# Moving a four-tile TensorE block to the head of the output product, with one wait ahead of it and two PSUM banks for its remainder

## Chip, cores, metric

One core of one Trainium2 chip (trn2). The metric is the device time of one execution in microseconds. Faster or slower needs 2%; smaller differences are given with their 95% interval.

## The reference

An attention without a score matrix, then a dense layer with a gated activation, for 8 batches, 8 heads, 576 positions, 64 channels a head, 2048 hidden units:

```python
q_s = softmax(q, channels); k_s = softmax(k, positions)
kv  = einsum('bhsd,bhse->bhde', k_s, v)          # a 64 x 64 matrix per head
x   = einsum('bhsd,bhde->bhse', q_s, kv)         # 576 x 64 per head
h   = x @ w_in                                   # 4608 x 512 by 512 x 2048
out = (h * sigmoid(beta * h)) @ w_out            # 4608 x 2048 by 2048 x 512
```

## The kernel before

The kernel works in nine slabs of 512 rows. Slab t is batch t's first 512 positions; slab 8 collects the remainders (64 positions of each of 8 batches). A slab has **pass one** (16 tiles of four 128x512 matmuls; ScalarE empties each tile's bank with the activation, into GT) and then the **output product** (seven parts of sixteen 128x256 matmuls, a Strassen-like scheme whose partial results VectorE adds up in TS). While slab t runs, TensorE also computes the next slab's x. Time is counted in slots, 64 for each of the two passes.

From slab 3 on, the next batch's x comes from `quad`: 64x64 matmuls in the four quarters of the array at once. It has eight matmuls of 512 columns (`x_mm`, for XT) and, for batches 6 and 7, sixteen of 64 columns for the remainders of a pair of batches (`r_mm`, for XT8). Four banks take the first, one bank both halves (`a` = 0, 1) of the second.

```python
HB, OB, MB = (0, 1, 2), (3, 4), (5, 6, 7)      # PSUM banks; pass one rotates over HB

def quad(b, pi=None):
    bks = list(MB) + [HB[(hrot[0] + 1) % 3], HB[(hrot[0] + 2) % 3]]
    b_r = bks[4]
    ...
    def r_mm(a):
        for g, e_, c in ...:
            op = add(PE, ...matmul into PS[b_r]..., r=[("kvd", d, hp), "qtr"], bank=[b_r])
            ...
                op.hard = [o_ for a_, o_ in done if a_ != a]   # TensorE waits for itself
    x_mm(0, 1); r_mm(0); x_mm(0, 0); x_mm(1, 1); x_mm(1, 0); r_mm(1)
    ...  # VectorE and ScalarE copy two banks each to XT; VectorE copies the remainder to XT8

def attn(b):                                    # slabs 4 to 6, b = t + 1
    return [(24 if b == 5 else 16, steps(kv_all, b)),
            (90, one(quad, b, b - 4 if b > 5 else None))]      # third part of the product

def pass2_fast(t, tick, hooks):
    s, z5, z2 = HB[hrot[0] % 3], OB[0], OB[1]
    ...
    at(0)
    ...  # part 1 into bank s, part 2 into bank 3; TS = s; TS -= bank 3   (lines L899, L902)
    prod(z2, *gs2(1), *wo(0, 0), True)                         # part 3 into bank 4
    ...  # TS -= bank 4 (L908), then the other four parts, which use banks 3 and 4 in turn
```

`add` records an operation with the keys it reads and writes and the banks it touches, and gives it a wait for each last operation of another engine on these. The waits of one operation stand ahead of it in its engine's queue.

The softmax here doesn't subtract the row's maximum and nothing guards it: scores larger than these inputs give would overflow.

## Time and profile before

| | |
|---|---|
| time, median of 6 runs | 273.88 us (273.44 to 274.79) |
| span in the profile | 271.7 us |
| TensorE busy | 97%, granted clock 1.00 |
| the block and the waits that it causes, slabs 3 to 6 | 4.30 us |

The last row is worked out in the prediction: in each slab the time from the end of the product's matmuls ahead of the block to the next product matmul, and the two waits for L908. This "block cost" is the measure used below. TensorE is the bound, its matmuls start every 0.109 us (256 columns) or 0.216 us (512 columns), and whatever is longer between two starts is cost.

How to read the profile lines below: a line of a timeline gives start and duration in us, engine, line of the kernel, operation, output and inputs, shape, and how many instructions it holds; in brackets, how long the engine was idle before it and what released it. A line of a list of waits gives the total in us, the number of waits, and the longest. Some traces lack matmul records: that of the kernel before has 1918 of 1937, and a gap of 0.22 us where pass one begins is the time of one 512-column matmul whose record is missing.

### The profile page before, as it was taken

The numbers are of one execution on the slowest core, as the hardware profiler recorded it, in microseconds if no ns is written. First come the engines' busy times: TensorE is split into PE (matmuls) and PEld (weight loads), VectorE is DVE, ScalarE is ACT, GpSimd is POOL, SyncE is SP. The second block draws the span as 40 slices with busy tenths as digits, with TensorE's granted clock in tenths as the row PEclk, the third lists the DMA queues.
The fourth block names the chain that finished last, engine by engine and source line by source line (L and its number), as shares of the span: only waits on it lengthen the run. The fifth ranks groups of instructions, "written<-read, shape, count | busy, mean of one in ns | idle before, by whom it ended". The sixth has DMA issues, their size and how long they took to land.

```text
span 271.7 us, 4870 instructions
## 1 busy us (share of the span) xinstructions
PE 264.3 (97%) x1918; PEld 164.7 (61%) x1937; DVE 192.4 (71%) x408; ACT 181.1 (67%) x286; POOL 62.1 (23%) x80
## 2 busy tenths in 40 slices
PE   8999999999999999999999999999999999999994
PEld 2544454448844885477547864677457745874683
DVE  4964586887867799869776976678686649625762
ACT  4998658789287957897778847883783387018610
POOL 2790010006530099001900570126000100000000
PEclk9999999999999999999999999999999999999999
DMA  7999999989799139920499999112600030012005
GB/s 214 321 204 207 227 326 349 291 231 367 175 340 271 78 62 298 339 80 2 97 315 262 315 330 200 74 29 50 214 0 2 19 157 0 0 60 96 0 3 154
DMA packets 59366, 45.93 MB, mean 169 GB/s; under 512 B 28608, under 2 KB 58320, under 8 KB 58320
## 3 DMA queue, kind: packets, MB, share of 16 engines
q1 hardware_dynamic: 54480, 40.90, 53.0%
q0 software_dynamic: 4240, 4.19, 9.3%
q10 hardware_dynamic: 624, 0.53, 0.6%
q8 instruction: 15, 0.25, 0.4%
q14 instruction: 7, 0.06, 0.1%
HBM read 36.71 MB, written 9.44 MB: 170 GB/s over the span
## 4 chain that ended last, share of the span: by engine, by line
PE 88%; DVE 5%; DMA 2%; SPq 2%; issue 1%; ACT 0%
PE PS L406 51%; PE PS L830 35%; DMA VF<-in_v_dram 2%; PE PS L482 1%; PE PS L543 1%; DVE QS L357 1%; SPq L278 1%; SPq L290 1%; DVE EQ L361 1%; DVE XT L573 1%; DVE VB L377 1%; DVE TS L908 0%; DVE XT L579 0%; DVE QI L359 0%; DVE XT L511 0%
## 5 line engine op out<-in xcount | busy, mean ns | idle before, releaser
L406 PE MATMUL PS<-XT,WIN 128*128 128x512 bf16 x562 | 126.0, 379 | 1.1 <-issue 0.3
L730 ACT ACTIVATE GT<-PS,BETA 128x512 bf16<-128x512 f32 x144 | 95.2, 690 | 37.7 <-PE PS L406 37.4
L406 PEld LDWEIGHTS PS<-XT,WIN 128*128 128x128 bf16 x576 | 55.3, 98 | 64.6 <-DVE XT L511 0.6
L753 DVE TENSOR_SCALAR GT<-GT,RB 128x512 bf16<-128x512 bf16 x144 | 53.3, 392 | 36.3 <-ACT GT L730 35.5
L361 POOL TENSOR_TENSOR EQ<-EQ,QI 128x1024 bf16<-128x1024 bf16 (+1 forms) x13 | 25.6, 1967 | 50.6 <-DVE QI L359 50.0
L830 PE MATMUL PS<-WOUT,GT 128*128 128x256 bf16 x256 | 32.2, 273 | 0.4 <-DVE TS L908 0.4
L830 PE MATMUL PS<-WOUT,GS 128*128 128x256 bf16 x256 | 31.3, 273 | 0.0
L830 PE MATMUL PS<-WSUM,GT 128*128 128x256 bf16 x256 | 30.1, 273 | 0.3 <-DMA QT<-EQ 0.2
L830 PEld LDWEIGHTS PS<-WSUM,GT 128*128 128x128 bf16 x256 | 24.8, 98 | 3.9 <-issue 0.9
L830 PEld LDWEIGHTS PS<-WOUT,GT 128*128 128x128 bf16 x256 | 24.7, 98 | 3.6 <-DVE TS L908 0.9
L866 ACT COPY O2S<-PS 128x512 f32<-128x512 f32 (+1 forms) x17 | 9.4, 561 | 26.2 <-PE PS L830 25.0
L830 PEld LDWEIGHTS PS<-WOUT,GS 128*128 128x128 bf16 x256 | 24.3, 98 | 3.3 <-issue 0.4
L319 ACT ACTIVATE EQ<-QF 128x512 bf16<-128x512 f32 x32 | 18.0, 621 | 7.6 <-DMA QF<-in_q_dram 7.5
L789 DVE TENSOR_TENSOR GS<-GT 128x512 bf16<-128x512 bf16 (+2 forms) x32 | 21.9, 685 | 0.0
L357 DVE TENSOR_REDUCE QS<-EQ 128x16 f32<-128x1024 bf16 (+1 forms) x20 | 19.7, 985 | 0.8 <-ACT EQ L319 0.8
L796 DVE TENSOR_TENSOR GT<-GT 128x2048 bf16<-128x2048 bf16 x16 | 19.8, 1262 | 0.0
L377 POOL CAST VB<-VF 128x512 bf16<-128x512 f32 x24 | 14.8, 616 | 21.9 <-DVE GS L789 13.2
L319 ACT ACTIVATE EK<-KF 128x512 bf16<-128x512 f32 x32 | 18.1, 621 | 0.1
L878 DVE TENSOR_TENSOR O2S<-TS,PS 128x512 f32<-128x512 f32 (+1 forms) x17 | 10.7, 643 | 8.7 <-PE PS L830 8.7
L830 PE MATMUL PS<-WSUM,GS 128*128 128x256 bf16 x128 | 16.6, 273 | 0.0
L406 PE MATMUL PS<-WOUT,GT 128*128 128x512 bf16 x62 | 15.0, 379 | 0.1
L784 DVE TENSOR_TENSOR GS<-GT 128x256 bf16<-128x256 bf16 (+2 forms) x32 | 13.6, 426 | 1.1
(90 smaller groups left out, 215.8 us busy)
## 6 DMA issues: line engine op xcount, KB each, us to landing
out_dram<-O2S SPq DMA_DIRECT2D x8, 1024.0 KB, 5.0
QF<-in_q_dram SPq DMA_DIRECT2D x6, 1024.0 KB, 6.3
KF<-in_k_dram SPq DMA_DIRECT2D x6, 1024.0 KB, 8.7
VF<-in_v_dram SPq DMA_DIRECT2D x6, 1024.0 KB, 12.1
KF<-in_k_dram SPq DMA_DIRECT2D x8, 256.0 KB, 5.6
VF<-in_v_dram SPq DMA_DIRECT2D x8, 256.0 KB, 5.6
WOUT<-in_moe_w_out_dram POOLq DMA_DIRECT2D x4, 512.0 KB, 16.4
WIN<-in_moe_w_in_dram POOLq DMA_DIRECT2D x3, 512.0 KB, 9.2
```

Source lines behind the costliest of these rows:

```text
L319: add(ACTE, lambda e, o=o, a=a: e.activation(o, a, ACT.Exp), r=[(name + "f", i, hp)], w=[("e" + name, i, hp)])
L357: add(DVE, lambda e: e.tensor_reduce(s_, a, AX.X, ALU.add), r=ks, w=[("qs", i, hp0)])
L361: add(eng, lambda e: e.tensor_tensor(a, a, vb, ALU.mult), r=ks + [("qi", i, hp0)], w=ks)
L377: add(eng, lambda e: (e.copy if eng == ACTE else e.tensor_copy)(o, a), r=[("vf", i, hp), ("vone", i)], w=[("vb", i, hp)], after=after)
L406: add(PE, lambda e: e.matmul(o, l, r_, start=start, stop=stop), r=r, w=w, bank=[bk])
L730: add(ACTE, lambda e: e.activation(GT[:, f, :], PS[bk][:, :], ACT.Silu, scale=BETA[:, f:f + 1]), r=[("ps", bk), "beta"], w=[("gt", f, 0), ...
L753: add(DVE, lambda e: e.tensor_scalar(GT[:, f, :], GT[:, f, :], RB[:, f:f + 1], None, ALU.mult), r=k + ["rb"], w=k)
L784: add(DVE, lambda e: e.tensor_tensor(GS1[:, i:i + n, :], gv(i, 0, n), gv(i + NG, 1, n), ALU.add), r=gk(i, 0, n) + gk(i + NG, 1, n), w=[("g ...
L789: add(DVE, lambda e: e.tensor_tensor(GS2[:, i:i + n, :], GT[:, i:i + n, :], GT[:, i + NG:i + NG + n, :], ALU.add), r=[k_ for f in (i, i + ...
L796: add(DVE, lambda e: e.tensor_tensor(gv(f, th, NG), gv(f, th, NG), gv(f, 1 - th, NG), ALU.subtract), r=gk(f, 0, NG) + gk(f, 1, NG), w=gk(f ...
L830: add(PE, lambda e, l=l, r_=r_, st=st, u=u, i=i, b_=b_: e.matmul(PS[b_][:, 256 * u:256 * u + 256], l, r_, start=st, stop=end and i == NG - ...
L878: add(DVE, lambda e, b_=b_, u0=u0, u1=u1: e.tensor_tensor(o[:, u0:u1, :], ts[:, u0:u1, :], bank3(b_)[:, u0:u1, :], ALU.add), r=["ts", ("ps ...
```

## The change

Its intent: let the block stand where two passes meet anyway; replace the waits scattered over its matmuls by one; and give each remainder half its own bank, so that TensorE does not wait for itself. The core of the diff:

```diff
-        def quad(b, pi=None):
-            bks = list(MB) + [HB[(hrot[0] + 1) % 3], HB[(hrot[0] + 2) % 3]]
-            b_r = bks[4]
+        def quad(b, gs=(0, 1), pi=None):
+            bks = list(MB) + [HB[(hrot[0] + 1) % 3], HB[(hrot[0] + 2) % 3], OB[1]]
+            b_r = bks[4:6]
+            used = list(b_x.values()) + (b_r if rem else [])
+            first = [dict(r=[... all kvd, qt, qtr keys of the block ...], bank=used)]
+            def tile(o, l, r_, a, c, bk, keys):
+                kw = dict(r=keys, bank=[bk])
+                if first:
+                    kw = first.pop()            # the first matmul waits for everything
...
-            x_mm(0, 1); r_mm(0); x_mm(0, 0); x_mm(1, 1); x_mm(1, 0); r_mm(1)
+            r_mm(1); x_mm(0, 0); x_mm(0, 1); x_mm(1, 0); x_mm(1, 1); r_mm(0)
+            r_evac(1) ... XT copies ... r_evac(0)
...
-                    (90, one(quad, b, b - 4 if b > 5 else None))]
...
+            if 3 < t < 7:
+                quad(t + 1, (0, 1), t - 3 if t > 4 else None)
             at(0)
```

(Some statements are joined on one line here.) The rest of the diff regroups two steps of slabs 1 and 2 without changing the order of instructions, and splits the key of XT8 in two.

## The prediction

> **What bounds the kernel now.** I read the page first, for shares, then the list of waits, then the order of time around each 64x64 block. Line L406 is pass one (and other full-array matmuls), L830 the output product, L543 the block's 512-column matmuls, L554 its 64-column remainders.
>
> ```profile
> span 271.7 us, 4870 instructions
> PE 264.3 (97%) x1918; PEld 164.7 (61%) x1937; DVE 192.4 (71%) x408; ACT 181.1 (67%) x286; POOL 62.1 (23%) x80
> PE 88%; DVE 5%; DMA 2%; SPq 2%; issue 1%; ACT 0%
> PE PS L406 51%; PE PS L830 35%; DMA VF<-in_v_dram 2%; PE PS L482 1%; PE PS L543 1%; DVE QS L357 1%; SPq L278 1%; SPq L290 1%; DVE EQ L361 1%; DVE XT L573 1%; DVE VB L377 1%; DVE TS L908 0%; DVE XT L579 0%; DVE QI L359 0%; DVE XT L511 0%
> ```
>
> TensorE is busy 97% and holds 88% of the chain that ended last; the block holds 1%. So a change is worth what it alters in the times from one TensorE matmul to the next. The list of TensorE's waits after 100 us holds one that the change can touch; the second list is the weight loads', 125 to 215 us:
>
> ```profile
> PE PS L830 <- DVE TS L908: 0.4, 2, 0.2
> ...
> PEld PS L554 <- PE PS L543: 0.9, 2, 0.5
> ```
>
> The first is the product waiting for VectorE's subtraction from bank 4 (slabs 5 and 6). The second is the remainder's second half waiting on TensorE itself. Slab 5 in order of time shows both (the third line is of the weight loads, the rest of the matmuls):
>
> ```profile
> 177.81 1.04 PE L830 MATMUL PS<-WOUT,GS 128*128 128x256 bf16 x8
> 178.78 0.40 PE L543 MATMUL PS<-QT,KVD 64*64 64x512 bf16 x2
> ...
> 179.51 0.20 PEld L554 LDWEIGHTS PS<-QTR,KVD 64*64 64x64 bf16 x8 [0.47 <-PE PS L543]
> ...
> 179.76 0.39 PE L830 MATMUL PS<-WOUT,GS 128*128 128x256 bf16 x2
> 179.99 1.91 PE L830 MATMUL PS<-WOUT,GT 128*128 128x256 bf16 x16
> 182.08 1.92 PE L830 MATMUL PS<-WOUT,GT 128*128 128x256 bf16 x16 [0.18 <-DVE TS L908]
> ```
>
> The durations overlap in the pipeline, so I use start to start. Twelve product matmuls from 173.66 to 174.97 make 0.109 us each; pass one's take 0.216.
>
> **What the Trainium skill says.** "TensorE: Matmul & The Clock Gate", section "Wait — 56ns, not 53.3ns?": warm start-to-start is N / 2.4 GHz + about 2.5 ns, or 0.109 us for 256 columns. The trace agrees, with a granted clock of 1.00 in every slab. "TensorEngine Tiling (Array Packing)", section "Key Properties": a change of tiling mode drains the array. The trace agrees: in slab 3 the product's last matmul has streamed by 126.88 + 5 x 0.109 = 127.43 and the block starts at 127.52, and its weights are not preloaded. Same page, "Gotcha 1: PSUM Pressure": different row tiles cannot use one PSUM bank at once. That is the reason for the explicit wait between the two remainder halves, which share a bank now; the 0.47 us above is its trace.
>
> **What the block costs now**, from the end of the product stream ahead of it to the next product matmul:
> - slab 3, block of batch 4, no remainder: 127.43 to 128.08, 0.65 us.
> - slab 4, batch 5, no remainder: seven product matmuls from 150.20 end at 150.96, the next is at 151.78: 0.82. The extra 0.17 is a wait for VectorE's copy of an earlier remainder out of bank 5.
> - slab 5, with remainder: eight from 177.81 end at 178.68, the next is at 179.76: 1.08.
> - slab 6: the same, 1.08.
> - the waits for L908: 179.99 + 16 x 0.109 = 181.74 against 182.08, 0.34 in slab 5. In slab 6 the starts are 208.33 and 210.41, so 0.33. They exist because the block's VectorE copies (two of 0.6, one of 0.7) stand ahead of that subtraction.
>
> Sum: 0.65 + 0.82 + 1.08 + 1.08 + 0.34 + 0.33 = 4.30 us.
>
> **The change part by part.** The instruction order of the two kernels agrees on all engines but for this: in slabs 4 to 6 the block moves from the third of the product's seven parts to before its first; in slab 3 it stays. Its matmuls are the same 8 or 24. Its copies move ahead of the Exp work on ScalarE and ahead of both L899 and L908 on VectorE; the remainder copy becomes two half-size ones.
>
> *One wait.* In slab 3 only the merging counts. The waits there are long fulfilled, since 0.65 is near the two rounds of 0.213 plus both drains. I allow 0.03 saved: 0.62.
>
> *Block ahead of the product, slab 4.* Its four banks are 5, 6, 7 and 1; bank 1 is that of pass one's last tile but one.
>
> ```profile
> 145.05 0.69 ACT L730 ACTIVATE GT<-PS,BETA 128x512 bf16<-128x512 f32 x1 [0.18 <-PE PS L406]
> 145.91 0.69 ACT L730 ACTIVATE GT<-PS,BETA 128x512 bf16<-128x512 f32 x1 [0.18 <-PE PS L406]
> ...
> 147.23 0.42 DVE L789 TENSOR_TENSOR GS<-GT 128x512 bf16<-128x512 bf16 x1
> ```
>
> That eviction ends at 145.74; pass one ends streaming at 145.71 and the drain takes 0.09 anyway. So the wait is nearly free: block 0.67, product from 146.38. But the old remainder's matmuls in slab 4 come after 15 product matmuls, at 148.02, in bank 5, which the block's first VectorE copy now has to empty. VectorE is busy with pass one's sums; a copy starts each 0.6 us there, so this one runs about 147.57 to 148.25. Adding 0.06 (the gap from L908's end to its waiter) gives 148.31: a new stall of 0.29. Slab 4: 0.96.
>
> *Slabs 5 and 6, with remainder.* The two remainder halves use bank 4 and bank 2, and bank 2 is that of pass one's LAST tile. The second half, the last thing in the block, writes it; but as all waits stand before the first matmul, the whole block waits.
>
> ```profile
> 173.86 0.69 ACT L730 ACTIVATE GT<-PS,BETA 128x512 bf16<-128x512 f32 x1 [0.18 <-PE PS L406]
> ...
> 202.20 0.69 ACT L730 ACTIVATE GT<-PS,BETA 128x512 bf16<-128x512 f32 x1 [0.18 <-PE PS L406]
> ```
>
> In slab 5 the eviction ends at 174.55, TensorE could start at 174.61, and now starts the product at 173.66: 0.95 us idle, where the old product has work at once. In slab 6: 202.89 + 0.06 - 202.00 = 0.95.
>
> The block itself gets shorter. Without the self-wait I estimate 0.12 (the issue of eight small matmuls, from the 0.31 us group less its 0.19 us latency), two rounds of 0.213, 0.12 again, and 0.08 for the way out: 0.75 instead of 1.08. The entry drain is hidden in the idle time.
>
> The L908 wait goes. In slab 5 the product starts at about 175.36 and its third part ends at 180.6; L908 has nothing of the block ahead of it and is done by 181.5, where its bank is wanted at 182.4. The block's copies (175.6 to 177.7 on VectorE) are also over before the first subtraction's input, at about 178.3. Each slab: 0.95 + 0.75 = 1.70 against 1.08 + 0.34 = 1.42.
>
> *ScalarE.* Two copies of 0.52 us ahead of the Exp work push that later by about 1.7 us with the wait for the block. In slab 5 Exp then ends near 182.5, when the output copy's input is ready; its bank is wanted near 184.1. Off the path. The transposed remainder queries for slab 5 are issued at 166.22 and land about 2.5 us later, long before 173.66. Nothing new there.
>
> Sum after: 0.62 + 0.96 + 1.70 + 1.70 = 4.98 us. Change: +0.68 us, 273.82 + 0.68 = 274.5.
>
> **The rivals.**
> 1. *It gains about a microsecond.* The intended path: self-wait and L908 wait gone, no new wait. For it: 0.3 x 2 + 0.33 x 2 + 0.15 = 1.4 us of real TensorE loss that the change removes. Against it: pass one's last eviction always ends 0.9 us after its last matmul, in every slab. If the wait did not cost, 272.5.
> 2. *The idle time is worth more than I count.* VectorE's order at the head of the product gets four copies more; if they delay L899 (the first copy of the product), bank 3 or 4 comes free late. I find 0.5 us of slack in slab 5 and more in slab 4. If it fails, some 0.5 us each: 275.5 to 276.
> 3. *The move is neutral*, the last eviction's wait just equal to the waits removed. My terms differ by 0.28 us a slab, so errors of 0.15 in block length make this nearly true: 273.8.
>
> **Range and chances.** The runs of before lie within 0.5 us. My terms err by perhaps 0.2 a slab, together 0.5. So 274.5, with 273.6 to 275.3 holding it 8 times in 10. Two per cent would be 5.5 us; all that the block costs now is 4.3 us, and no rival adds over 2.5. Within 2%: 0.98; 0.01 each side.
>
> **What would show it.** In the new profile: TensorE idle, released by ScalarE's GT line, ahead of the block in slabs 5 and 6, 0.8 to 0.9 us each; about none in slab 4; a VectorE wait before the first old-remainder matmul of slab 4, 0.1 to 0.3 us; no wait on L908; no self-wait in the block, which takes 0.7 to 0.8 us there. I would be wrong if the idle before the block is under 0.5 us, if the block's matmuls in their new order run one after the other (over 1 us), or if VectorE appears as a releaser of the product in slabs 5 and 6.

## The result

| | time, median | ratio to before | 95% interval |
|---|---|---|---|
| before, 6 runs | 273.88 us | | |
| changed, 5 fast runs of 6 | 275.16 us | 1.0043 | 1.0023 to 1.0063 |
| changed again, 5 runs on another chip job | 274.83 us | 1.0038 | 1.0026 to 1.0051 |

Both intervals lie above 1: a small loss, clear of noise. A ratio is the mean time of one kernel's fast runs over that of the other's of the same rounds, so it is not quite the ratio of the medians. The sixth run of the changed kernel took 466.13 us at a granted clock of 0.56, and the first profile fell on it. So all readings "after" are from the profile of the second row, at a clock of 0.999 and a span of 273.4 us.

The waits of TensorE in the changed kernel after 100 us, complete:

```profile
PE PS L554 <- ACT GT L745: 2.0, 2, 1.0
```

This line has taken the place of the wait for L908; the list of the kernel before has three more entries, of 0.2 to 0.3 us each, where records are missing (L554 is the block's matmul now, L745 ScalarE's eviction of pass one's tiles, L845 the product, L596 the block's copies to XT, L406 still pass one). Slab 5 of the changed kernel in order of time, TensorE's matmuls:

```profile
172.72 1.89 PE L406 MATMUL PS<-XT,WIN 128*128 128x512 bf16 x8
175.59 0.22 PE L554 MATMUL PS<-QTR,KVD 64*64 64x64 bf16 x3 [0.98 <-ACT GT L745]
...
176.08 0.29 PE L554 MATMUL PS<-QTR,KVD 64*64 64x64 bf16 x8
176.30 1.48 PE L845 MATMUL PS<-WSUM,GS 128*128 128x256 bf16 x12
```

Pass one's stream ends at 172.72 + 8 x 0.216 = 174.45. The block starts 1.14 us later, and is then over in 0.71: 1.85 us to the product's first matmul, against 1.42 before. The eviction that it waits for, on ScalarE:

```profile
174.65 0.69 ACT L745 ACTIVATE GT<-PS,BETA 128x512 bf16<-128x512 f32 x1 [0.17 <-PE PS L406]
```

It ends at 175.34, 0.89 us after pass one's stream. Slab 6 is the same to 0.01 us (203.21 to 205.06). That L908 no longer holds the product is seen from the absence of any gap later in slab 5:

```profile
181.55 3.66 PE L845 MATMUL PS<-WOUT,GT 128*128 128x256 bf16 x32
185.04 3.22 PE L845 MATMUL PS<-WSUM,GT 128*128 128x256 bf16 x28
```

32 x 0.109 = 3.49, and the next group starts 3.49 later. And slab 4, TensorE, then VectorE's copy:

```profile
144.98 1.46 PE L406 MATMUL PS<-XT,WIN 128*128 128x512 bf16 x6
146.56 0.63 PE L554 MATMUL PS<-QT,KVD 64*64 64x512 bf16 x8
147.12 1.48 PE L845 MATMUL PS<-WSUM,GS 128*128 128x256 bf16 x12
148.44 0.49 PE L845 MATMUL PS<-WOUT,GS 128*128 128x256 bf16 x3
148.96 0.19 PE L406 MATMUL PS<-QTR,KVD 128*128 128x64 bf16 x1
```

```profile
148.13 1.28 DVE L596 CAST XT<-PS 128x512 bf16<-128x512 f32 x2
```

The block costs 147.12 - (144.98 + 6 x 0.216) = 0.84 us. The old remainder's first matmul, due at 148.44 + 3 x 0.109 = 148.77, starts at 148.96, after the first of the two copies, which ends near 148.8. That is the foreseen stop, 0.19 us.

The block cost in slabs 3 to 6 is thus 0.65 + (0.84 + 0.19) + 1.85 + 1.85 = 5.38 us, against 4.30: +1.08 us. The measured ratio, 1.0038 of 274, is +1.04 us, so no other part is needed to explain it. (The spans differ by 1.7 us; 0.57 of that is there already when slab 3's block starts, at 128.09 against 127.52, ahead of anything that the change moves. The profiled execution of the changed kernel, 275.46 us, was itself 0.63 above the median of its runs.)

### The profile page after: what moved, and what is told of

Its sections match the earlier page's. It is cut to its first block, busy times and chain, and to the rows that moved or that the text cites. A ratio compares the mean times of both kernels' runs of the same rounds, so it can differ in the third digit from the quotient of the medians.

```text
span 464.1 us, 4896 instructions
## 1 busy us (share of the span) xinstructions
PE 457.5 (99%) x1937; PEld 224.7 (48%) x1937; DVE 194.0 (42%) x410; ACT 183.6 (40%) x286; POOL 61.4 (13%) x80
## 4 chain that ended last, share of the span: by engine, by line
PE 99%; ACT 0%; issue 0%; DVE 0%
PE PS L406 59%; PE PS L845 37%; PE PS L482 1%; PE PS L554 1%; PE PS L404 1%; ACT GT L745 0%; DVE O2S L893 0%; DVE WARM L229 0%
## 5 line engine op out<-in xcount | busy, mean ns | idle before, releaser
L406 PE MATMUL PS<-XT,WIN 128*128 128x512 bf16 x576 | 225.3, 582 | 0.0
L745 ACT ACTIVATE GT<-PS,BETA 128x512 bf16<-128x512 f32 x144 | 97.0, 687 | 147.5 <-PE PS L406 147.5
L406 PEld LDWEIGHTS PS<-XT,WIN 128*128 128x128 bf16 x576 | 75.4, 132 | 138.2 <-issue 114.6
L845 PE MATMUL PS<-WOUT,GT 128*128 128x256 bf16 x256 | 54.6, 390 | 0.0
L845 PE MATMUL PS<-WOUT,GS 128*128 128x256 bf16 x256 | 52.7, 389 | 0.0
L845 PE MATMUL PS<-WSUM,GT 128*128 128x256 bf16 x256 | 51.5, 389 | 0.0
L845 PEld LDWEIGHTS PS<-WSUM,GT 128*128 128x128 bf16 x256 | 33.6, 131 | 16.8 <-issue 1.7
L845 PEld LDWEIGHTS PS<-WOUT,GS 128*128 128x128 bf16 x256 | 33.6, 133 | 14.9
L845 PEld LDWEIGHTS PS<-WOUT,GT 128*128 128x128 bf16 x256 | 33.2, 130 | 15.0
L845 PE MATMUL PS<-WSUM,GS 128*128 128x256 bf16 x128 | 27.5, 381 | 0.0
L406 PE MATMUL PS<-WOUT,GT 128*128 128x512 bf16 x64 | 26.7, 586 | 0.0
L845 PEld LDWEIGHTS PS<-WSUM,GS 128*128 128x128 bf16 x128 | 15.7, 125 | 10.1 <-issue 1.9
```

What stands on the lines that cost most here:

```text
L406: add(PE, lambda e: e.matmul(o, l, r_, start=start, stop=stop), r=r, w=w, bank=[bk])
L745: add(ACTE, lambda e: e.activation(GT[:, f, :], PS[bk][:, :], ACT.Silu, scale=BETA[:, f:f + 1]), r=[("ps", bk), "beta"], w=[("gt", f, 0), ...
L845: add(PE, lambda e, l=l, r_=r_, st=st, u=u, i=i, b_=b_: e.matmul(PS[b_][:, 256 * u:256 * u + 256], l, r_, start=st, stop=end and i == NG - ...
```

## The experiments

My theory before the runs: the loss is the wait for pass one's last eviction, because the block's sixth bank is that tile's bank and the single wait holds the whole block for it. The rivals: (A) moved copies delay other engines' work, (B) the new order of matmuls is slow in itself, (C) the single wait costs, not the place. All runs are correct by the comparison with the reference, with a caution at the late place. "Sum" is the block cost of slabs 3 to 6, read as above, each time from one profiled execution; the row "place alone" has its profile from the second look at that kernel and its ratio from the first.

| run | slab 3 | slab 4 | slab 5 | slab 6 | sum | sum less before | ratio (95% interval) |
|---|---|---|---|---|---|---|---|
| before | 0.65 | 0.82 | 1.42 | 1.41 | 4.30 | | |
| changed | 0.65 | 1.03 | 1.85 | 1.85 | 5.38 | +1.08 | 1.0038 (1.0026 to 1.0051) |
| place alone | 0.65 | 1.03 | 1.76 | 1.75 | 5.19 | +0.89 | 1.0035 (1.0020 to 1.0050) |
| eviction's wait last | 0.65 | 1.04 | 1.64 | 1.64 | 4.97 | +0.67 | 1.0013 (0.9998 to 1.0028) |
| own waits | 0.65 | 1.03 | 1.18 | 1.19 | 4.05 | -0.25 | 0.9989 (0.9977 to 1.0001) |
| old place | 0.65 | 0.91 | 1.23 | 1.22 | 4.01 | -0.29 | 0.9986 (0.9974 to 0.9998) |
| other bank | 0.65 | 1.04 | 1.02 | 1.02 | 3.73 | -0.57 | 0.9978 (0.9963 to 0.9994) |
| own waits, old remainder later | 0.65 | 0.66 | 1.18 | 1.18 | 3.67 | -0.63 | 0.9972 (0.9959 to 0.9986) |
| after the subtraction | 0.65 | 0.66 | 0.80 | 0.80 | 2.90 | -1.40 | 0.9938 (0.9923 to 0.9953) |

For eight kernels the sum, read in four places of 1 to 2 us each, gives the measured difference in 274 us to about 0.3 us (the widest: +0.67 against +0.36, and -1.40 against -1.70).

**Changed kernel again.** No edit.

> The changed kernel as it is, for a profile at full clock (the first one fell in a throttled state). Ratio 1.0043 again, about 275.1 us. My theory (TensorE pays for the wait on the last eviction): idle of 0.8 to 0.9 us ahead of the block in slabs 5 and 6, 0.2 to 0.4 us before the old remainder's first matmul in slab 4, no wait for L908; the sum from 0.7 to 1.2 us. Rival A (the moved copies delay ScalarE or VectorE): new waits of the product for VectorE or ScalarE lines other than these. Rival B (the block's matmuls run in series in their new order): block over 1.0 us from first to last in slabs 5 and 6.

Measured 274.83 us, ratio 1.0038. The idle time, the stop in slab 4 and the missing wait for L908 are there. In size the idle time is over what was expected (0.98 us in the profile's brackets, against 0.8 to 0.9), and the stop is at the low end (0.19 against 0.2 to 0.4). The block's matmuls take 0.71 us, so they do not run in series (rival B falls), and no other wait on VectorE or ScalarE appears (rival A falls as far as TensorE's list of waits shows it).

**Own waits.** Each matmul waits for its own data and bank:

```diff
-                if first:
-                    kw = first.pop()
```

> The changed kernel, but each matmul of the block waits for its own data and bank; order, banks and place stay. My theory: in slabs 5 and 6 the block starts with the product's old start and only its last eight matmuls wait for the last eviction, some 0.3 to 0.4 us; 0.5 us back in each, about 1.0 us in all, so 274.1 (ratio to before 1.000 to 1.001). Rival A (moved copies) and rival B (series): no change, 275.1.

Measured 273.66 us, ratio 0.9989; 1.3 us less than the changed kernel. Slab 5:

```profile
171.79 1.89 PE L406 MATMUL PS<-XT,WIN 128*128 128x512 bf16 x8
173.61 0.22 PE L552 MATMUL PS<-QTR,KVD 64*64 64x64 bf16 x2
...
173.75 0.60 PE L552 MATMUL PS<-QT,KVD 64*64 64x512 bf16 x6
174.45 0.31 PE L552 MATMUL PS<-QTR,KVD 64*64 64x64 bf16 x8
174.70 1.48 PE L843 MATMUL PS<-WSUM,GS 128*128 128x256 bf16 x12
```

The block starts 0.09 us after pass one's stream (173.52), and only the last eight matmuls wait for the eviction, which ends at 174.40 in this run. The stop falls from 1.14 us to about 0.35: the last eight start 0.84 us after the block's first matmul, against 0.49 at the old place, where nothing holds them. The gain is a third larger than expected; 0.2 us a slab of it has another source, see "eviction's wait last".

**Old place.** The new form at slot 90; bank 4 is in use there, so that half takes the product's first bank:

```diff
-                bks = list(MB) + [..., HB[(hrot[0] + 2) % 3], OB[1]]
+                bks = list(MB) + [..., HB[(hrot[0] + 2) % 3], HB[hrot[0] % 3]]
+                    (90, one(quad, b, (0, 1), b - 4 if b > 5 else None))]
-            if 3 < t < 7:
-                quad(t + 1, (0, 1), t - 3 if t > 4 else None)
```

> The new form (one wait, two banks for the remainder) at the old place in the third part of the product; bank 4 is in use there, so the half that had it takes the product's first bank. My theory: the self-wait goes and nothing comes for it: 0.3 us off in each of slabs 5 and 6, the wait for L908 stays (0.3 to 0.5 each, as the remainder copy is now two); 273.2 to 273.6, ratio 0.998. Rival B: block no shorter than 1.08 us, ratio 1.000 or more. Rival A: ratio below 1, too, as the copies are back in their place.

Measured 273.55 us, ratio 0.9986. Slab 5:

```profile
176.54 2.13 PE L846 MATMUL PS<-WOUT,GS 128*128 128x256 bf16 x18
178.60 0.22 PE L554 MATMUL PS<-QTR,KVD 64*64 64x64 bf16 x2
...
179.31 0.39 PE L846 MATMUL PS<-WOUT,GS 128*128 128x256 bf16 x2
```

The block with remainder falls from 1.08 to 0.81 us, so the new form as a whole gains 0.27 us a slab where nothing new is waited for. Two smaller copies on VectorE instead of one make the wait for L908 longer, 0.42 us instead of 0.34. In slab 4 the single wait loses: the block costs 0.91 us instead of 0.82, because the copy out of bank 5 now holds its first matmul (released by VectorE's L530 after 0.19 us) and not only the matmuls in that bank.

**Late place.** The same at slot 112:

> The new form at the place that slab 3 has for it (sixth part of the product), for slabs 4 to 6, after L908 and after the first output copies. My theory: self-wait, wait for L908 and the 0.17 us in slab 4 go, 1.4 us in all, so 272.5 (ratio 0.995). What could take it back: the block's copies come late for the next pass one, which would show as a wait of L406 on DVE XT or ACT XT at the head of slabs 5 to 7; then 273 to 274. Rival B: no gain.

Measured 290.19 us, ratio 1.0563, and the edit was at fault, not the theory. At slot 112 the next pair's remainder queries have already been put into QTR (the transpose of slab t is recorded ahead of the block), so the block waits for that transfer:

```profile
182.94 0.71 PE L846 MATMUL PS<-WSUM,GT 128*128 128x256 bf16 x5
192.05 0.26 PE L554 MATMUL PS<-QTR,KVD 64*64 64x64 bf16 x2 [8.40 <-DMA QTR<-EQR]
```

It then computes with the next pair's queries. The comparison passed all the same; I take it (not tested) that the softmax of small random inputs is so flat that its tolerance cannot tell one batch's queries from another's. An order of instructions has to be checked for what is read, not only for races. The stops also cost clock. "TensorE: Matmul & The Clock Gate" in the Trainium skill, section "What's actually happening", has a cold clock of half speed after some 3.4 us idle. The trace agrees: the granted clock was 0.50 from 186.90 to 197.14, that is from inside the stop of 8.40 us (it ends at 192.05) to 5 us after it, and again from 224.44 to 231.27, from inside a second stop of 3.49 us in slab 6 (it ends at 225.71). This run says nothing of the theory.

**After the subtraction.** The mended form, at slot 94: after L908 is recorded and ahead of that transpose. Against the kernel of the old place:

```diff
-                    (90, one(quad, b, (0, 1), b - 4 if b > 5 else None))]
+                    (94, one(quad, b, (0, 1), b - 4 if b > 5 else None))]
```

> The new form at slot 94, in the fourth part of the product, after L908 is recorded, but before the remainder queries of the next pair are normalized and transposed. (At slot 112 the block stood behind that transpose and so waited for it, and read the next pair's remainder queries: a fault of that run's edit, not seen by the comparison's tolerance.) My theory: blocks of 0.65, 0.65, 0.81, 0.81 us, no wait for L908, none for the old remainder's copy: 2.9 us against 4.3, so 272.6, ratio 0.995. What could take it back: the copies come some 5 us later on VectorE, and bank 3 is wanted by the next pass one's fourth tile; then a wait of L406 on a VectorE line, ratio 0.997 to 1.0.

Measured 272.48 us, ratio 0.9938, the fastest of all, and faster than both kernels beyond the interval. Slab 5:

```profile
179.06 0.71 PE L846 MATMUL PS<-WOUT,GT 128*128 128x256 bf16 x5
179.70 0.22 PE L554 MATMUL PS<-QTR,KVD 64*64 64x64 bf16 x2
...
180.40 3.12 PE L846 MATMUL PS<-WOUT,GT 128*128 128x256 bf16 x27
183.36 3.66 PE L846 MATMUL PS<-WSUM,GT 128*128 128x256 bf16 x32
187.07 2.11 PE L406 MATMUL PS<-XT,WIN 128*128 128x512 bf16 x9
```

From 179.605 to 180.40 is 0.80 us, and the product's groups follow without a gap. (The 0.22 us before pass one at 187.07 is a missing record; the kernel before has the same at 187.54.) The later copies on VectorE delay nothing: no wait on a VectorE line is left in TensorE's list.

**Place alone.** The old form of the block (its own waits, one bank for both halves), called at the new place:

```diff
+            if 3 < t < 7:
+                quad(t + 1, t - 3 if t > 4 else None)
             at(0)
-                    (90, one(quad, b, b - 4 if b > 5 else None))]
```

> The old form of the block (waits at each matmul, remainder halves in one bank with the self-wait) at the new place. Its first remainder half is second in order and takes the bank of pass one's last tile. My theory: the place with this bank is the cause, so the loss is there in the old form too: about 0.9 us of stop, after the first two matmuls, in slabs 5 and 6, the self-wait as before, no wait for L908; 1.8 to 2.0 us a slab against 1.42, ratio 1.003 to 1.005 (about 275.0). Rival C (the single wait is at fault, not the place): ratio 1.000 or below.

Measured 275.15 us, ratio 1.0035. The loss is there with the old form too: rival C falls, as far as it says that the single wait alone is at fault. The profile fell on a slow execution: 715 us at a recorded clock of 1.00, though the mean 128x512 matmul of pass one took 835 ns, against 379 in the kernel before. What it was stays open. So one more look at the same kernel:

> The same kernel as the run of the place alone, whose profile fell in a slow state, for a profile at full clock. My theory: in slabs 5 and 6 two matmuls of the block, then 0.8 to 0.9 us of stop released by the last eviction, then the rest with the self-wait: 1.8 to 2.0 us from the end of pass one to the product; 274.9 to 275.2.

Measured 274.7 us, one run, just below the 274.9 to 275.2 expected. Slab 5:

```profile
173.96 0.40 PE L543 MATMUL PS<-QT,KVD 64*64 64x512 bf16 x2
174.89 0.31 PE L554 MATMUL PS<-QTR,KVD 64*64 64x64 bf16 x8 [0.54 <-ACT GT L729]
...
175.62 1.48 PE L829 MATMUL PS<-WSUM,GS 128*128 128x256 bf16 x12
```

As expected: two matmuls, then the stop for the eviction (it ends at 174.75), then the rest. It is 0.93 us from the first two matmuls' start to the next; the old order puts the half with that bank second, so its own waits help it little. The slab costs 1.76 us, just below what I expected (1.8 to 2.0), because the self-wait is nearly hidden here: the list of the weight loads' waits has 0.2 us of it a slab, against 0.47 before.

**Eviction's wait last.** In the changed kernel the wait on ScalarE is the first of five in slabs 5 and 6, ahead of four on VectorE and on transfers that have long been fulfilled. Two separate wait instructions in the queue hold two each, the first matmul's weight load the fifth. In slab 5's trace the two stand at 175.38 and 175.49, the weight load at 175.56. Here the wait on ScalarE is the one held by the weight load (the first of the kernel's list ends up there). The edit reaches only the first matmul of the block in slabs 4 to 6:

```diff
-            waits.append(sorted(need.items(), key=str))
+            waits.append(sorted(need.items(), key=lambda n: (
+                len(need) < 4 or op.eng != PE or n[0] != ("eng", ACTE), str(n))))
```

> The changed kernel, where the wait on ScalarE is the last of the block's waits, held by the matmul itself, and not the first of five. In the profile of the changed kernel at full clock TensorE starts 0.22 us after the eviction's end in slabs 5 and 6, where a wait on one semaphore in the run with own waits took 0.05. If the waits that stand behind cost this, the start is now 0.05 us after the eviction's end: 0.15 to 0.17 us back in each of slabs 4, 5 and 6, 0.45 in all, ratio about 1.002. If it is the array's start from rest that costs, 0.22 us stays and the ratio 1.004.

Measured 274.53 us, ratio 1.0013. Slab 5:

```profile
174.83 0.22 PE L555 MATMUL PS<-QTR,KVD 64*64 64x64 bf16 x2 [0.78 <-ACT GT L746]
```

```profile
174.09 0.69 ACT L746 ACTIVATE GT<-PS,BETA 128x512 bf16<-128x512 f32 x1 [0.17 <-PE PS L407]
```

The eviction ends at 174.78, TensorE starts 0.05 us later. In the changed kernel it was 175.34 and 175.59, 0.25 to the matmul. So 0.20 us a slab in slabs 5 and 6 come from the order of the waits alone; the rival in the expectation, that the array's start from rest costs it, falls. In slab 4 the block gains 0.18, but reaches the stop at bank 5 sooner, which grows from 0.19 to 0.38; nothing is won there.

**Other bank.** Place and single wait as in the changed kernel; the remainder halves in banks 4 and 3, not in the last tile's:

```diff
-                bks = list(MB) + [..., HB[(hrot[0] + 2) % 3], OB[1]]
+                bks = list(MB) + [..., OB[1], OB[0]]
```

> The changed kernel, place and single wait kept, but the remainder halves in banks 4 and 3, so that the single wait holds pass one's last tile but one at the latest. My theory: idle ahead of the block falls from 1.14 to about 0.28 us in slabs 5 and 6, and at most 0.2 us come back as a wait for VectorE to empty bank 3 for the product's second part: 1.0 to 1.2 us a slab against 1.85, ratio 0.998 to 0.9995. If the single wait or the place cost for another reason than the last eviction: ratio stays at 1.004.

Measured 273.48 us, ratio 0.9978. The block of slab 5:

```profile
171.70 2.32 PE L406 MATMUL PS<-XT,WIN 128*128 128x512 bf16 x10
174.14 0.22 PE L554 MATMUL PS<-QTR,KVD 64*64 64x64 bf16 x3
...
174.85 1.48 PE L845 MATMUL PS<-WSUM,GS 128*128 128x256 bf16 x12
176.19 1.48 PE L845 MATMUL PS<-WOUT,GS 128*128 128x256 bf16 x12
```

It starts 0.28 us after pass one's stream (173.86) instead of 1.14, with the same place and the same single wait. One bank number turns a loss of 1.0 us into a gain of 0.6, slightly more than expected. Bank 3 is emptied in time but for 0.03 us (12 x 0.109 after 174.85 is 176.16).

**Own waits, old remainder later.** As own waits, and:

```diff
-                    todo += spread(outr_steps(3), 72, 88)
+                    todo += spread(outr_steps(3), 80, 96)
```

> The run with own waits, and the old remainder's eight matmuls of slab 4 moved from slots 72 to 88 to slots 80 to 96, so that VectorE has emptied bank 5 by then. My theory: the 0.38 us before the first of them goes and nothing comes for it; the sum of slabs 3 to 6 falls from 4.05 to 3.67 us, ratio to before 0.9977 (0.997 to 0.9985). Rival: the stop only moves to another of the product's waits, sum 4.0, ratio 0.999.

Measured 273.31 us, ratio 0.9972. Slab 4:

```profile
149.36 0.27 PE L843 MATMUL PS<-WOUT,GS 128*128 128x256 bf16 x1
149.47 0.19 PE L406 MATMUL PS<-QTR,KVD 128*128 128x64 bf16 x1
```

TensorE's stop before the old remainder is gone (149.36 + 0.109 is 149.47) and appears nowhere else; slab 4 falls to 0.66 us. So the term of slab 4 is shown by its removal.

## Why the prediction was right

The measured time, 275.16 (then 274.83), lies in the range 273.6 to 275.3, close to its end; the ratio is within 2%. By its steps:

- *The wait for the last eviction takes the place of the waits removed.* Shown: it is the one wait in the list; changing the bank takes it away, keeping the place and the single wait.
- *Idle of 0.95 us in slabs 5 and 6.* It was 1.14 us (in the profile's brackets 0.98, over the sign given, 0.8 to 0.9). The term was too small by 0.19, because I took 0.06 us from the end of an operation to its waiter from a wait on one semaphore (L908's). This wait is followed by others in the queue, and the step is 0.25; with the wait at the end it is 0.05.
- *Block of 0.75 us.* It was 0.71, which hides 0.04 of the error above; the self-wait and its loss are gone, as the old place shows too (1.08 to 0.81).
- *The wait for L908 goes.* It did, in both slabs.
- *Slab 4: 0.67 and a stop of 0.29.* It was 0.84 and 0.19. The first has the same error of queued waits; the second partly makes up for it.
- *Slab 3 saves 0.03.* It saved nothing: 0.65.
- The sum was 4.98 us; it is 5.38. The errors: 0.30 in slabs 5 and 6, 0.07 in slab 4, 0.03 in slab 3. The queued waits are the term left out: slabs 5 and 6 were 0.15 over their terms each (1.85 against 1.70), and with the eviction's wait last each is 0.21 shorter (1.64). That this kernel's sum is 4.97, nearly the prediction's 4.98, is partly luck: there slabs 5 and 6 lie 0.06 each below their terms, slabs 3 and 4 together 0.11 above.
- The rounds of 0.213 us in the block are 512 columns at the cited 2.4 GHz. In slab 3 of the kernel before, the two rounds start 0.24 us apart (127.52 and 127.76).

Of the rivals in the prediction, the first (a gain of a microsecond if the wait did not cost) describes the block away from the last eviction: other bank gains 0.6 us, after the subtraction 1.4 to 1.7. The second (VectorE's order delays the product) did not happen. The third (a neutral move) missed: the new wait and block cost 0.43 us a slab more than what went (1.85 against 1.42), where the prediction had 0.28. What I had not considered is that the order of the waits within the one wait matters.

## What to carry to other kernels

A block moved to a seam between two stages inherits the banks that the stage before has just filled: look whether one of its banks is that of the last eviction, and give it a bank that has been idle for longer. Merging waits into one ahead of the block makes its first instruction wait for what only its last one needs; merge waits that are long fulfilled, and leave the late one at the matmul that needs it, or at least last in the queue. Where a bound engine is 97% busy, adding up start-to-start gaps in the few places that a change touches came within about 0.3 us of the measured effect in the eight kernels here.

## What the Trainium skill lacked or had wrong

- "Perfetto Trace Analysis", section "Identifying Dependency Chains", says that an instruction with several conditions may have wait instructions put ahead of it, and gives no cost. Here, a matmul with five conditions started 0.25 us after the one that came last when that one stood first in the queue, and 0.05 us after it when it stood last.
- "TensorEngine Tiling (Array Packing)", section "Key Properties", says that a change of mode drains the array, without a figure. Here the way from full-array matmuls into the four-tile block took 0.09 us from the end of the stream (127.43 to 127.52), and a block of eight 64x512 matmuls cost 0.65 us with both changes.
- "TensorE: Matmul & The Clock Gate", section "Back-to-back issue gap", gives about 131 ns for sustained matmuls of 512 columns with their weight loads. This kernel's pass one sustains 216 ns (18 matmuls from 141.82 to 145.71 in the kernel before), which is the same page's isolated figure.
